# When the beacon keys of the last five sequences are loaded, cast and turned, in a fused attention and MLP kernel

## The chip, the cores and the metric

The kernel runs on one core of one Trainium2 chip. The metric is device time in microseconds (us) of one execution, and the time before is the median of three runs. A profile is one execution recorded by the hardware profiler. The engines are PE (TensorE matmul; its weight loads are shown as PEld), DVE (VectorE), ACT (ScalarE), POOL (GpSimd) and SP (SyncE, which here only issues DMAs). Every engine works through its own list of instructions in order.

## The reference

The first half is attention over 8 sequences with 8 heads of 64, 576 tokens each. Ahead of the causal keys stand 16 "beacon" keys and values per head that every token sees. The second half is an MLP over the 4608 tokens.

```python
k_all = np.concatenate([beacon_k, k], axis=2)          # 16 + 576 keys, B=8, H=8, D=64
v_all = np.concatenate([beacon_v, v], axis=2)
scores = scale * np.matmul(q, k_all.transpose(0, 1, 3, 2))
scores = np.where(causal, -1000000000.0, scores)       # no mask on the beacons
...
x = np.ascontiguousarray(attn_out.transpose(0, 2, 1, 3)).reshape(B * S, H * D)
h = x @ w_in                                           # 512 -> 2048
g = np.maximum(0.01 * h, h)
return (g @ w_out).astype(np.float32)                  # 2048 -> 512
```

## The kernel before

**Tiling.** Two heads make a pair, so there are 32 pairs, g = 0 to 31, four to a sequence. A pair's keys stand in one of eight buffers, `k_bufs[g % 8]`, as 64+64 rows (two heads) by 592 columns: 16 beacon columns first, then the 576 keys. Scores are made transposed, keys by queries, in 64-row matmuls (`score` at L267 for pairs 0 to 7, `stretch` at L314 for pairs 8 to 31); ACT takes the exponential (L276, L329, L333); POOL zeroes the causal triangles (`triangle`, L289; called the masks here); the value matmuls (L359) also give the sums, and DVE divides (L388, L389). The MLP runs in nine chunks of 512 tokens between these steps: `up` is one 128-column piece of the first product (L442, then ACT's Prelu at L450), `down` a piece of the second (L519 for the first chunk, L544 after it, in a seven-product scheme whose sums DVE makes at L785).

**How keys get into place.** For pairs 8 and up, `load_natural` (N, L171) issues two DMAs on POOL's queue for q (N g.0) and two for k (N g.1), which also cast to bf16; `turn_pair` (T, L179) issues two DMA transposes on SP's queue that write qT and columns 16 to 591 of the key buffer. `load_v_cast` (L209, L214) loads values on POOL's queue.

**Beacon keys.** They take a path of their own. `load_beacon_k(b0, b1, eng)` (L185) loads a range of sequences as fp32, 128 partitions (head, beacon) by sequence by 64, one packet of 256 bytes for each row. `cast_beacon_k` (L188) casts to bf16. `beacon_transposes` (L194) does two PE transposes for each sequence into one PSUM tile, and DVE copies the result in two halves into `bkT` (L203). `beacon_columns` (step b, L229) is a POOL copy of 16 columns of `bkT` into pair g's key buffer. Sequences 0 and 1 (pairs 0 to 7) go a separate, early way, and the rest, sequences 2 to 7 (pairs 8 to 31), are loaded, cast and turned together.

**The order of work.** Up to pair 7 the order is written out by hand in strings that `run` reads: s score, m mask, v value, x finish, l, N and V loads, T turn, q and k transposes on PE, b beacon columns, u up, d down, o a half of w_out. From pair 8 (`FIRST`) on, the order is a list of events, each with a due time counted in pairs and a priority; `block(m)` is three score tiles of 512 columns for each head with their masks behind them. The list is sorted, and before each event the loop calls `fill()`, which emits ups and downs until their count reaches what is due at that time. So an event's time says between which ups and downs PE meets it, and in which order POOL, DVE and SP meet their own parts. Pair 12 first appears in block 4 (due 12.09), pair 13 in block 5 (13.02), pair 14 in block 6 (13.94) and pair 15 in block 7 (14.86).

**PSUM.** One pool, `ps_one`, has four banks. Ups, values, the first tile of each block (two banks) and the transposes share them in turn: a new tile takes the bank of the fourth tile before it and waits until that has been read out.

Of the kernel before, what the change touches and what calls it, by code (L numbers as in the profile page):

```python
# [15 lines left out]
def kernel(  # L16
# [11 lines left out]
    nc = tc.nc  # L28

    B, H, S, D = q.shape  # L30
# [5 lines left out]
    NPAIR = H // 2  # L36
# [80 lines left out]
    def make_pads():  # L117
        nc.vector.memset(k_all[:, :, NB + S :], 0.0)
        for t in a_bufs:
            for c in PADS:  # L120
                nc.vector.memset(t[:, :, c : c + 48], 0.0)

    def make_ones():
        for t in v_bufs:
            nc.vector.memset(t[:, :, :, D : D + 1], 1.0)
# [37 lines left out]
    def load_first_keys():  # L163
        for h in range(2):
            nc.sync.dma_start(out=first_k[h], in_=k[0, h].rearrange("(p i) d -> p i d", i=RI))
# [18 lines left out]
    def load_beacon_k(b0, b1, eng):  # L184
        eng.dma_start(out=bk_raw[:, b0:b1], in_=beacon_k[b0:b1].rearrange("b h n d -> (h n) b d"))  # L185

    def cast_beacon_k(b0, b1, copy):
        copy(out=bk[:, b0:b1], in_=bk_raw[:, b0:b1])  # L188

    def beacon_transposes(b0, b1):  # L190
        ps = ps_one.tile([128, 1024], BF16, name="tp", tag="one")
        for b in range(b0, b1):
            for par in range(2):
                nc.tensor.transpose(  # L194
                    ps[par * 64 : par * 64 + 64, (b - b0) * 128 : (b - b0 + 1) * 128], bk[:, b], ident
                )
        for par in range(2):
            ps_ = slice(par * 64, par * 64 + 64)
            src = ps[ps_, 0 : (b1 - b0) * 128].rearrange("p (x e n) -> p e x n", e=2, n=NB)[:, par]
            if b0 == 0:  # L200
                nc.vector.tensor_copy(out=k_all[ps_, :, 0:NB], in_=src)
            else:
                nc.vector.tensor_copy(out=bkT[ps_, b0:b1].rearrange("p b h n -> p (b h) n"), in_=src)  # L203
# [134 lines left out]
    def triangles(parts):  # L338
        for g, lo, hi in parts:
            for c in range(NKB):  # L340
                n = (112, 128, 128, 128, 80)[c]
                if lo < FLAT[c] + n <= hi:
                    triangle(probs[g], FLAT[c], n, ROWS[c])
# [167 lines left out]
    def ND(i):  # L511
        return NF if i == 0 else 2 * len(PRODUCTS)
# [308 lines left out]
    def unused(n, cols=128):  # L821
        ps = ps_one.tile([128, 512], FP32, name="av", tag="one")
        r, w = max(1, cols // 128), min(cols, 128)
        for i in range(n):
            nc.tensor.matmul(
                out=ps[:, 0 : r * w].rearrange("p (r w) -> p r w", w=w),
                lhsT=blank,
                rhs=blank[:, None, 0:w].to_broadcast([128, r, w]),
                start=True,
                stop=True,  # L830
            )
# [82 lines left out]
    with order:  # L914
        load_first_keys()
        load_beacon_k(0, 2, nc.scalar)
        nc.vector.memset(blank, 0.0)
        nc.vector.memset(ident, 0.0)
        run("l0.0 l1.0")
        make_identity(nc, ident, nomemset=True)  # L920
        make_ones()
        run("l1.1 l2.0 l2.1 V0.0 V0.1 l3.0 l3.1 V0.2 V0.3 V0.4 l4.0 l4.1 i0")
        make_pads()
        unused(13, 256)
        cast_beacon_k(0, 2, nc.scalar.copy)
        beacon_transposes(0, 2)
        unused(13)
        nc.scalar.copy(out=k_nat0[:, :, 0], in_=first_k[0])
        nc.vector.tensor_copy(out=k_nat0[:, :, 1], in_=first_k[1])
        run("q0.1 k0 w2.384 s0.0 m0.0 w3.256 s0.1 q1 s0.2 m0.1 k1 s0.3 m0.2")  # L930
        run("w2.384 s1.0 m1.0 q2 s1.1 k2 w2.384 s1.2 m1.1 w2.384 s1.3 m1.2 W0.0.4 s2.0 m2.0 W0.0.4 s2.1 W0.0.6 q3 l5.0 l5.1 s2.2 k3 w4.384 v0.0 m2.1 s2.3 i1 m2.2 W0.1.4 s3.0 m3.0 v1.0 s3.1 v0.1 s3.2 v1.1 m3.1 l6.0 l6.1 s3.3 x0.1 m3.2")
        run("v2.0 V1.0 V1.1 q4 v2.1 x1 k4.1 v3.0 v3.1 x2.1 s4.0 s4.1 x3 m4.0 V1.2 V1.3 V1.4 l7.0 l7.1 u u s4.2 s4.3 q5 k5 m4.1 m4.2 u o0 u")
        load_beacon_k(2, B, nc.gpsimd)
        run("s5.0 s5.1 m5.0 u u u s5.2 s5.3 q6 k6 m5.1 m5.2 o1 u u s6.0 s6.1 m6.0 u v4.0 u v4.1 y4 N8.0 N8.1 u s6.2 s6.3 q7 k7 m6.1 m6.2 u")
        cast_beacon_k(2, B, nc.gpsimd.tensor_copy)
        run("u v5.0 u v5.1 N9.0 s7.0 s7.1 m7.0 d x5 v6.0 v6.1 T8 d s7.2 s7.3")
        beacon_transposes(2, B)
        run("m7.1 m7.2 N9.1 u b8.2 b9.2 b10.2 b11.2 x6 v7.0 T9 v7.1 d d d N10.0 N10.1 d V2.0 V2.1 x7 t0 T10")


        FIRST = 2 * NPAIR
        COLS = FLAT[NKB]
        TILES = (NG - FIRST) * COLS // 512

        def tile_parts(n):
            at, end, parts = 512 * n, 512 * (n + 1), []
            while at < end:
                r, lo = divmod(at, COLS)
                hi = min(COLS, lo + end - at)
                parts.append((FIRST + r, lo, hi))  # L950
                at += hi - lo
            return parts

        def block(m):
            tiles = [tile_parts(n) for n in range(3 * m, min(3 * m + 3, TILES))]
            for n, parts in enumerate(tiles):
                stretch(parts, apart=n == 0)
            for parts in tiles:
                triangles(parts)

        def has_down():
            return at2[0] < done1[0] // NF

        since = 0
        events = []
        for g in range(FIRST, NG):
            if g > FIRST + 2:
                events.append((g - 3.25, 0, run, ("N%d.0" % g,)))
                events.append((g - 2.95, 0, run, ("N%d.1" % g,)))
            if g > FIRST + 2:  # L970
                events.append((g - 1.75, 0, run, ("T%d" % g,)))
            if g > FIRST + 3:
                events.append((g - 2.5, 0, run, ("b%d.2" % g,)))
            at = g + (2.05 if g % NPAIR == NPAIR - 1 else 2.25)
            events.append((at, 3, value, (g, 0)))
            events.append((at + 0.37, 4, value, (g, 1)))
            if g < NG - 1:
                events.append((at + 0.38, 5, x_turn, (g,)))
        for m in range((TILES + 2) // 3):
            events.append((FIRST + (0.4 if m else 0.6) + 1536 / COLS * m, 2, block, (m,)))  # L980
        ends = [FIRST]
        for g in range(FIRST, NG):
            at = g + (2.5 if g == NG - 1 else 3.5)
            events.append((at, 2, finish, (g, 2)))
            if g % NPAIR == NPAIR - 1:
                ends.append(at)
        for at, n in ((NG - 1.2, 5), (NG - 0.3, 6), (NG + 0.7, 4)):
            events.append((at, 7, w_in_sums, (n,)))
        for b in range(2, B):
            for n in range(2 if b == 2 else 0, NKB):  # L990
                events.append((4 * b + ((-0.1, 0.1)[n > 3] if b == 2 else 0.3 * n - 0.4), 6, load_v_cast, (b, n)))
        events.sort(key=lambda e: e[:2])
        first_down[0] = 4
        w, d0 = 0, done1[0] + done2[0]
        for at, _, what, args in events:
            while w + 2 < len(ends) and at > ends[w + 1]:
                w, d0 = w + 1, done1[0] + done2[0]
            todo = NF * ready[0] + sum(ND(i) for i in range(ready[0])) - (KEPT if w + 2 < len(ends) else LEFT) - d0
            aim = d0 + todo * (at - ends[w]) / (ends[w + 1] - ends[w])
            while done1[0] + done2[0] < aim and fill():  # L1000
                pass
            if what is block:
                since = done1[0] + done2[0]
            elif what is value:
                while done1[0] + done2[0] < since + (2 if has_down() else 4) and fill(True):
                    pass
            what(*args)
        assert at2 == [TAIL - 1, ND(TAIL - 1) - LEFT] and done1[0] == TAIL * NF, (at2, done1)
        apart_from_values[0] = True
        last_chunks("D X31 x7 d a1 R111 x8 R111 t u d u d u d u u d u d u u w")  # L1010
        last_chunks("R111 R111 R111 t u d u d u d u d d d14")
# [30 lines left out]
```

## Time and profile before

| what | value |
|---|---|
| median of three runs (lowest, highest) | 325.34 us (325.18, 329.55) |
| the profiled execution's own time | 325.64 us |
| its span, first to last instruction | 323.8 us |
| time outside of the span | 1.84 us |
| granted TensorE clock | 1.00 |
| PE busy | 314.3 us (97%) |
| POOL busy | 184.3 us (57%) |
| ACT busy | 203.8 us (63%) |
| packets on POOL's DMA queue | 99824 |

The span is what lies between the first and the last instruction. Busy times are a union over an engine's instructions. A timeline line has the start, the time covered, engine, line, operation, tile written and tile read, shape and count, and in brackets the idle time before it and what ended that. Times in it are from the start of the span. In the chain of waits, a line is a start, a length and what the time belonged to.

### The profile page before, as it was taken

What the parts mean: (1) busy time and instruction counts of PE and PEld (TensorE: products, weight loads), DVE (VectorE), ACT (ScalarE), POOL (GpSimd) and SP (SyncE); (2) the same over time, 40 slices, a digit from 0 to 9 for tenths busy, and PEclk for the clock granted to TensorE, in tenths of its full rate; (3) what the DMA queues carried; (4) which work ended last, traced back from release to release, by engine and by line L of the source; (5) the groups of instructions that cost most, each with busy time, mean ns of one, the idle gap of its engine ahead of it and who ended that gap; (6) DMA issues with size and microseconds to landing.
All of it is one profiled execution on the core that took longest, in us unless ns stands there. A gap on an engine that the chain in (4) does not pass through costs nothing.

```text
span 323.8 us, 8701 instructions
## 1 busy us (share of the span) xinstructions
PE 314.3 (97%) x3468; PEld 219.1 (68%) x3494; DVE 168.0 (52%) x341; ACT 203.8 (63%) x346; POOL 184.3 (57%) x354
## 2 busy tenths in 40 slices
PE   7999999999999999999999999999999999999995
PEld 4575555444588557855788888656875697688784
DVE  3464245508255244444443454525464689577954
ACT  4968962387855786478746874687458547455510
POOL 8895868999996787659875977666221000000000
PEclk9999999999999999999999999999999999999999
DMA  8999999999999999999999999999222100200123
GB/s 137 129 189 192 124 214 140 169 177 188 135 152 160 216 138 129 114 186 97 141 176 174 99 143 119 188 128 129 44 81 82 26 2 32 75 25 2 65 67 130
DMA packets 155256, 39.78 MB, mean 123 GB/s; under 512 B 142368, under 2 KB 152480, under 8 KB 155216
## 3 DMA queue, kind: packets, MB, share of 16 engines
q0 software_dynamic: 99824, 18.54, 91.1%
q1 hardware_dynamic: 55120, 20.62, 38.3%
q8 instruction: 27, 0.44, 0.6%
q14 instruction: 13, 0.11, 0.1%
q10 hardware_dynamic: 272, 0.07, 0.1%
HBM read 37.22 MB, written 9.44 MB: 144 GB/s over the span
## 4 chain that ended last, share of the span: by engine, by line
PE 72%; DMA 14%; POOL 9%; ACT 3%; issue 1%; DVE 0%; POOLq 0%; ACTq 0%; SPq 0%
PE acc L442 24%; PE acc L544 19%; PE sc L544 11%; PE av L359 6%; PE sc L314 5%; PE acc L663 5%; DMA w_out_sb<-in_moe_w_out_dram 4%; DMA gsum<-in_k_dram 4%; POOL aT L289 3%; DMA k_nat<-in_k_dram 3%; DMA v_aug<-in_v_dram 2%; ACT aT L333 2%; DMA kT<-k_nat 2%; POOL gsum L158 1%; POOL v_aug L214 1%
## 5 line engine op out<-in xcount | busy, mean ns | idle before, releaser
L442 PE MATMUL acc<-xT,w_in_sb 128*128 128x512 bf16 (+1 forms) x537 | 116.5, 354 | 1.5 <-ACT aT L329 0.3
L450 ACT ACTIVATE gT<-acc 128x512 bf16<-128x512 f32 x124 | 70.8, 623 | 33.1 <-PE acc L442 32.6
L289 POOL TENSOR_SCALAR_AFFINE_SELECT aT<-aT 128x256 bf16<-128x256 bf16 (+2 forms) x160 | 59.7, 403 | 51.4 <-ACT aT L329 31.5
L442 PEld LDWEIGHTS <-w_in_sb 128*128 128x128 bf16 x560 | 51.7, 98 | 43.9 <-issue 2.9
L544 PEld LDWEIGHTS <-gT 128*128 128x128 bf16 x512 | 48.7, 98 | 7.7 <-issue 1.8
L333 ACT ACTIVATE aT<-sc 128x1024 bf16<-128x1024 f32 (+3 forms) x64 | 51.7, 892 | 0.0
L329 ACT ACTIVATE aT<-sc 128x512 bf16<-128x512 f32 (+3 forms) x64 | 29.0, 520 | 27.8 <-PE sc L314 27.8
L388 DVE RECIPROCAL rec<-av 128x6 f32<-128x6 f32 (+1 forms) x64 | 12.0, 187 | 65.0 <-PE av L359 64.4
L359 PEld LDWEIGHTS <-aT 128*128 128x128 bf16 (+1 forms) x960 | 36.9, 98 | 9.2 <-issue 1.4
L544 PEld LDWEIGHTS <-gsum 128*128 128x128 bf16 x384 | 36.5, 98 | 6.5 <-issue 0.4
L359 PE MATMUL av<-v_aug,aT 128*128 128x65 bf16 (+1 forms) x960 | 39.8, 194 | 0.8 <-DMA v_aug<-in_v_dram 0.4
L214 POOL DMA_DIRECT2D v_aug<-in_v_dram x40 | 34.1, 856 | 4.2 <-DMA w_in_sb<-in_moe_w_in_dram 3.8
L171 POOL DMA_DIRECT2D k_nat<-in_k_dram x48 | 34.8, 730 | 0.9 <-DMA w_out_sb<-in_moe_w_out_dram 0.3
L171 POOL DMA_DIRECT2D q_nat<-in_q_dram x48 | 34.8, 729 | 0.6 <-issue 0.4
L389 DVE TENSOR_TENSOR x_nat<-av,rec 128x384 bf16<-128x384 f32 (+1 forms) x64 | 31.4, 491 | 2.2
L544 PE MATMUL acc<-w_out_sb,gT 128*128 128x256 bf16 x240 | 28.9, 273 | 0.4 <-ACT gT L450 0.4
L276 ACT ACTIVATE aT<-sc 128x1024 bf16<-128x1024 f32 (+3 forms) x32 | 26.0, 874 | 4.7 <-PE sc L267 2.5
L314 PE MATMUL sc<-qT,kT 64*128 64x80 bf16 (+22 forms) x384 | 22.2, 250 | 0.3
L314 PEld LDWEIGHTS <-kT 64*128 64x128 bf16 x384 | 12.8, 94 | 11.2 <-issue 7.6
L544 PE MATMUL acc<-w_sum,gsum 128*128 128x256 bf16 x160 | 20.1, 273 | 0.0
L575 ACT COPY p<-acc 128x512 f32<-128x512 f32 x15 | 9.1, 604 | 16.8 <-PE acc L544 16.8
L785 DVE TENSOR_TENSOR gsum<-gT 128x1024 bf16<-128x1024 bf16 x16 | 11.0, 688 | 15.7 <-ACT gT L450 15.7
(95 smaller groups left out, 339.0 us busy)
## 6 DMA issues: line engine op xcount, KB each, us to landing
out_dram<-p SPq DMA_DIRECT2D x26, 256.0 KB, 3.2
q_nat<-in_q_dram POOLq DMA_DIRECT2D x48, 72.0 KB, 5.5
k_nat<-in_k_dram POOLq DMA_DIRECT2D x48, 72.0 KB, 5.3
v_aug<-in_v_dram POOLq DMA_DIRECT2D x24, 128.0 KB, 6.5
w_in_sb<-in_moe_w_in_dram POOLq DMA_DIRECT2D x2, 1024.0 KB, 12.4
w_out_sb<-in_moe_w_out_dram POOLq DMA_DIRECT2D x2, 1024.0 KB, 12.1
out_dram<-u SPq DMA_DIRECT2D x8, 256.0 KB, 2.7
gsum<-in_q_dram POOLq DMA_DIRECT2D x8, 144.0 KB, 7.1
```

The source lines that it names most:

```text
L171: nc.gpsimd.dma_start(out=t[:, :, par], in_=(q, k)[which][b, 2 * hp + par].rearrange("(t p) d -> p t d", p=NR),)
L214: nc.gpsimd.dma_start(out=dst[lo : ROWS[c], c, :, 0:D], in_=v[b, :, OFF[c] : OFF[c] + n].rearrange("h p d -> p h d"),)
L276: nc.scalar.activation(out=aT[:, :, c0 : c0 + w], in_=sc[:, :, 0:w], func=AF.Exp, scale=0.125)
L289: nc.gpsimd.affine_select(out=view, in_=view, compare_op=ALU.is_ge, fill=0.0, base=128 - n if lo == 0 else 0, channel_multiplier=-1, patte ...
L314: nc.tensor.matmul(out=(sc[par] if apart else sc[:, par])[:, at : at + b - a], lhsT=kT[ps_, c * 128 : (c + 1) * 128], rhs=qT[ps_, q0 : q0 ...
L329: nc.scalar.activation(out=probs[g][:, par, lo:hi], in_=sc[par][:, at : at + hi - lo], func=AF.Exp, scale=0.125)
L333: nc.scalar.activation(out=probs[g][:, :, lo:hi], in_=sc[:, :, at : at + hi - lo], func=AF.Exp, scale=0.125)
L359: nc.tensor.matmul(out=avv[:, n, 0 : D + 1], lhsT=aT[0 : ROWS[c], par, a0 : a0 + 128], rhs=va[0 : ROWS[c], c, 2 * hp + par, :], start=(c = ...
L389: nc.vector.tensor_tensor(out=x_nat[:, t0:t1].rearrange("p t e d -> p (t e) d"), in0=avv[:, :, 0:D], in1=rec[:, n0:n1, None].to_broadcast( ...
L442: nc.tensor.matmul(out=acc[:, lo:hi], lhsT=w_in_cols(fc, j), rhs=xT[:, j, x0 : x0 + hi - lo], start=(j == 0), stop=(j == NJ - 1), skip_gro ...
L450: nc.scalar.activation(out=gT[i][:, fc, :], in_=acc, func=AF.Prelu, alpha=0.01)
L544: nc.tensor.matmul(out=acc[:, lo : lo + HD], lhsT=left(i, n, fc, tile), rhs=right(n, fc), start=(lo == 0 and fc == 0), stop=(fc == HF - 1) ...
```

## The change

The early load, cast and turn take sequence 2 alone (pairs 8 to 11). Sequences 3 to 7 get a second load, due at 9.85 (in POOL's list between the q and the k loads of pair 13, N13.0 and N13.1), a second cast, due at 11.45 (in POOL's list behind the masks of block 3), and second transposes with their DVE copies, due at 11.6 (in PE's list between the two halves of pair 9's values). The beacon columns of pairs 12 to 15, which were due 2.5 pairs ahead of their pair, are due 0.38 ahead, since `bkT` is filled only now; those of pairs 16 and up stay where they were. Work as such is the same, apart from one DMA, one cast, one PSUM tile and two DVE copies more, each of these on fewer columns than the single one before.

```diff
-        load_beacon_k(2, B, nc.gpsimd)
+        load_beacon_k(2, 3, nc.gpsimd)
...
-        cast_beacon_k(2, B, nc.gpsimd.tensor_copy)
+        cast_beacon_k(2, 3, nc.gpsimd.tensor_copy)
...
-        beacon_transposes(2, B)
+        beacon_transposes(2, 3)
...
             if g > FIRST + 3:
-                events.append((g - 2.5, 0, run, ("b%d.2" % g,)))
+                events.append((g - (2.5 if g >= FIRST + 2 * NPAIR else 0.38), 0, run, ("b%d.2" % g,)))
...
+        events.append((FIRST + 1.85, 0, load_beacon_k, (3, B, nc.gpsimd)))
+        events.append((FIRST + 3.45, 0, cast_beacon_k, (3, B, nc.gpsimd.tensor_copy)))
+        events.append((FIRST + 3.6, 0, beacon_transposes, (3, B)))
         events.sort(key=lambda e: e[:2])
```

## The prediction

> **What bounds the kernel now.** I read the page first: busy times, slices and queues.
>
> ```profile
> PE 314.3 (97%) x3468; PEld 219.1 (68%) x3494; DVE 168.0 (52%) x341; ACT 203.8 (63%) x346; POOL 184.3 (57%) x354
> ...
> POOL 8895868999996787659875977666221000000000
> ...
> DMA  8999999999999999999999999999222100200123
> ...
> q0 software_dynamic: 99824, 18.54, 91.1%
> ```
>
> PE is the bound: 9.5 of 323.8 us are not PE's, and they include the head and the tail. So a microsecond that PE stands still is a microsecond of the end, and work that moves within PE's list costs nothing. But POOL and the DMA engines are full for the first two thirds, which is where the change works. Next, the chain of waits there.
>
> ```profile
> 39.96 13.69 DMA w_out_sb<-in_moe_w_out_dram
> ...
> 64.21 8.28 DMA k_nat<-in_k_dram
> 72.49 0.02 SPq L179
> 72.51 0.03 issue
> 72.54 5.26 DMA kT<-k_nat
> 77.80 0.05 issue
> 77.85 0.67 PE sc L314 x10
> ```
>
> Up to 77.85 the chain runs through POOL's loads; from there on nearly all is PE. So what could be won lies ahead of 77.85, and only as far as PE really waits. The timeline of PE, PEld's row among it:
>
> ```profile
> 77.12 1.39 PE L314 MATMUL sc<-qT,kT 64*128 64x96 bf16 x16
> 77.84 0.39 PEld L314 LDWEIGHTS <-kT 64*128 64x128 bf16 x10 [0.32 <-DMA kT<-k_nat]
> 81.91 1.13 PE L359 MATMUL av<-v_aug,aT 128*128 128x65 bf16 x30
> 83.83 0.83 PE L314 MATMUL sc<-qT,kT 64*128 64x224 bf16 x12
> 90.28 0.85 PE L314 MATMUL sc<-qT,kT 64*128 64x16 bf16 x16
> ```
>
> Block 3 (77.12) waits 0.32 us for pair 11's turned keys: the late transfer is worth only that. 81.91 is pair 9's values, both halves (12 and 18 matmuls, 0.031 us each, the second half from 82.32), where the new transposes go between. 83.83 is block 4, which needs pair 12; 90.28 is block 5, which needs pair 13. Last, the timeline of POOL:
>
> ```profile
> 48.15 0.50 POOL L188 CAST bk<-bk_raw 128x384 bf16<-128x384 f32 x1 [2.78 <-DMA bk_raw<-in_beacon_k_dram]
> ...
> 53.94 0.72 POOL L171 DMA_DIRECT2D k_nat<-in_k_dram  x1 [0.34 <-DMA w_out_sb<-in_moe_w_out_dram]
> ...
> 80.53 1.38 POOL L289 TENSOR_SCALAR_AFFINE_SELECT aT<-aT 128x256 bf16<-128x256 bf16 x4
> 81.87 0.19 POOL L229 COPY kT<-bkT 128x16 bf16<-128x16 bf16 x1
> ```
>
> POOL has no idle time between 72.6 and 97.6: each thing put into its list there makes all behind it later. The 80.53 row is block 3's masks, behind which the new cast stands.
>
> **The early stage.** Ten of twelve transposes leave 50.73 (0.45 us for twelve, start to start, so 0.0375 each): PE is 0.37 us ahead. The load has 128 packets in place of 768. By the landings of single issues, the first half of w_out lands at 47.26, the beacon load at 48.09, so its 768 packets take 0.83 us; 640 fewer are 0.69 us. The cast still waits for that landing behind w_out, until about 47.4; what POOL wins there is lost again at 51.70, where it waits for ACT (0.92 us). The wait at 53.94 is for the second half of w_out, issued eight POOL DMAs earlier and landed at 53.65; it then lands near 52.96, and POOL, free at 53.60, goes on 0.34 sooner. Two more waits look the same, for loads issued eight before: 0.28 us at 69.53 (landing 69.24) and 0.17 at 72.61 (landing 72.32). Loads land 0.34 to 0.69 sooner, I take 0.5, so pair 13's second q load is issued at 72.0 in place of 72.61, with pair 12's copy (a step of 0.13) gone too. Pair 11's keys are turned at 77.3 in place of 77.80. Block 0 (61.15, right behind pair 8's turned keys at 61.06) moves with its keys. So PE is 0.5 us ahead behind block 3: the gain so far.
>
> **The load.** One more issue on POOL, ahead of pair 13's k. The value load of 640 packets (64.93) takes 0.76 us on POOL, bounds 0.53 (beacon values, 58.06) and 0.85 (today's 768 packets). It goes out at 72.73. Issues from 71.71 to 74.05 landed after 4.97 to 5.73 us, so it lands at 77.7 to 78.5, more than 3 us ahead of the cast. The transfers behind it lose the 0.69 us again, to about today's times: pair 13's keys were turned at 89.18, and block 5 asks for them past 90.5. SP's list gets nothing new.
>
> **A rule against the load.** The DVE sums at L468 to L470 took 1.22 to 1.23 us each (57.98 to 61.71), and the five POOL issues that start beside them (58.06 to 61.02) 0.53 to 0.91 as elsewhere, so I add nothing for DVE. The Trainium skill, "SBUF — State Buffer", section "SBUF: two separate sides", says that a DVE operation holding the port pair it shares with GpSimd keeps GpSimd from writing descriptors. By that the issue beside the L472 sum could wait up to 2.30 us, and the total would be about 3 us in place of 0.65; the five issues speak against it. What did collide there is a mask: the third of block 2's (75.41) took 1.44 us beside L472, its kind elsewhere 0.38. POOL and DVE shift against each other now, so those 1.05 us stay or go; I keep them, and take the other end for a rival.
>
> **The cast.** At the end of block 3's masks POOL is 0.61 ahead, less 0.76 for the load, plus 0.13 for pair 13's copy, which goes: 0.02 late, so the cast starts at 81.89. It costs 0.50 x 320/384 = 0.42 us (bounds 0.19, the smallest POOL copy, and 0.50): done 82.31, seen by PE about 0.05 later as at 77.80 to 77.85, and 82.40 with rounding up.
>
> **The transposes.** PE is done with the first half of pair 9's values at 82.28 - 0.5 = 81.78 and now waits 0.6 us: POOL, not PE, sets this point. Behind the wait stand the second half, one up and block 4. Ten transposes take 0.375 us, so the second half starts at 82.78, where it was 82.32: the gain of 0.5 is gone and 0.46 us are lost. Its PSUM bank is that of the third up instead of the second; ACT read that out at 82.76 at the latest, and now sooner, so nothing is added. DVE's two copies (0.36 each for 384 columns, so at most 0.7) end near 83.55. Behind them on DVE stands the second half's division, which SP's x transposes take at 84.81 (it was done at 83.82; covered).
>
> **Pair 12 to 15's columns.** Behind the cast come two value loads (82.00 to 83.34), then pair 12's copy, 83.65 to 83.84. Block 4 needs it at 84.06 + 0.46 = 84.52: covered by 0.68. POOL is now 0.44 late (0.42 cast, 0.02). Pair 13's copy stood at 77.53 and now stands behind block 4's masks and two value loads: today's 89.70, plus 0.44, plus the load of 0.86, so 91.00 to 91.19. Block 5's fifth group of matmuls, which needs it, was at 90.59, now 91.05; with 0.05 to be seen, PE waits 0.19. Pair 14's copy comes at 96.6 to 96.8, block 6 needs it past 97.4; for pair 15 POOL has had idle time since 97.6. Block 4's masks get 0.44 late, but pair 11's values, which need them, come 4 us later.
>
> **Sum.** +0.46 + 0.19 = 0.65 us. Nothing behind absorbs it: PE's own wait rows sum to 4.0 us over the whole span, and most of that is ahead of 78. On the profiled execution that is 325.64 + 0.65 = 326.3; the median lies 0.30 below that execution, so 326.0. A measurement of this kernel tells about 2% (6.5 us) from no change, so I call this the same.
>
> **A rule on splitting.** The packets take 0.83 us per 768 between landings that follow each other, so cutting one load in two adds only the issue. The Trainium skill, "DMA: Bandwidth & Descriptors", section "Anatomy of one DMA — SWDGE (gpsimd) path", gives each DMA a fixed 2 us, mostly completion; as occupancy it would make the sum about 2.6, and landings half a microsecond apart (54.33, 54.69, 55.32, 55.70) say it is not that.
>
> **Rival 1, the relief pays.** If the 1.05 us of the slow mask go, POOL no longer sets the point: block 3's last mask then waits for ACT (81.29 - 0.5), the cast ends near 81.7, PE does not wait, the second half starts at its bank's release, 82.76 - 0.5 = 82.26, and pair 13's copy is in time. That is -0.06, so 325.3; and if the DMAs land the full 0.69 sooner with no bank in the way, at best -0.6, 324.7. For it: rows of 0.38 for that mask everywhere else. Against: POOL is full. Chance 0.33.
>
> **Rival 2, the landing takes the place of the cast's early wait (slower).** The load's own row today is 10.65 us to land, waiting at 48.15 for 2.78. At 72.73 + 10.65 = 83.38 POOL would stand 1.5 us at the cast, PE with it, and pair 13's copy goes as late: 0.65 + 1.5 = 2.15, 327.5. With the longest landing of the trace, 13.69, it is 5.2, 330.5. It decides from 9.2 us on (81.89 - 72.73). Against: issues from 60 to 100 landed within 8.83. Chance 0.1.
>
> **Rival 3, POOL's copies late one after another.** If the load and cast cost their upper ends (0.09 and 0.08 more) and one more mask collides for 1.05, PE waits 1.2 more at the transposes and pair 13's stall stays: 1.9, 327.2. Chance 0.1.
>
> **How the numbers follow.** The forecast's own case (0.2 to 1.5 us slower, 325.5 to 326.8) gets 0.47, the rivals 0.33, 0.1 and 0.1. The range goes from rival 1's best, 324.7, less 0.2 as runs scatter, 324.5, to rival 2's first price, 327.5, with 0.3 for scatter (median to profiled execution): 327.8. Left out are rival 2 with longer landings and a run disturbed like the 329.55 one. Over 2% slower needs 6.5 us, which only rival 2's worst with rival 3's 1.25 on top would reach: 0.03, out of theirs. Over 2% faster would need more than PE's waits hold: 0.01.
>
> **What will show it.** Right: PE's transposes in two places, the second behind a wait on POOL's cast of some tenths; the wait for pair 11's kT smaller; POOL's row at 53.94 without its wait; the cast with no DMA wait. Wrong: a cast that waits for its load; transposes with no wait (rival 1); masks of 1.4 us in new places; a wait of block 4 on pair 12's copy; or landings that did not move.

## The result

The changed kernel is slower by a little: over 22 runs of each, 1.0047 of the time before, with a 95% interval of 1.0027 to 1.0066. The medians are 327.08 and 325.27 us. The medians count every execution, the ratio leaves out the slow ones (more than 1.5% above the kernel's fastest). At 325.3 us the ratio is 1.5 us, from 0.9 to 2.1. That is inside 2% and slower, as forecast, but more than twice the 0.65 us of the prediction, which lies below the interval.

The page of the changed kernel, in the lines that answer to those shown of before:

```profile
PE 321.2 (98%) x3468; PEld 222.0 (67%) x3494; DVE 168.1 (51%) x343; ACT 204.5 (62%) x346; POOL 185.1 (56%) x356
...
POOL 8857874999998778756966887678221000000000
...
DMA  8999999999999999999999999999422100100123
...
q0 software_dynamic: 99856, 18.54, 81.2%
```

In this one execution PE's matmuls were much slower up to about 24 us, ahead of every instruction that the change touches (two unused matmuls of 384 columns took 0.82 us, in before 0.50; the profile's granted clock is 1.00 in both). Its span is 329.3 us, so the readings below use a second profile of the same kernel, e_again, with a span of 325.0 us. The counts of the page hold: two POOL instructions, two DVE copies and 32 packets more.

The timeline of PE in e_again (start, time covered, instructions, idle time before):

```profile
76.84 0.34 PE L314 MATMUL sc<-qT,kT 64*128 64x96 bf16 x6
77.82 0.67 PE L314 MATMUL sc<-qT,kT 64*128 64x128 bf16 x10 [0.63 <-DMA kT<-k_nat]
81.88 0.53 PE L359 MATMUL av<-v_aug,aT 128*128 128x65 bf16 x12
82.34 0.47 PE L194 MATMUL tp<-ident,bk 128*64 128x128 bf16 x10
82.78 0.71 PE L359 MATMUL av<-v_aug,aT 128*128 128x65 bf16 x18
84.29 0.83 PE L314 MATMUL sc<-qT,kT 64*128 64x224 bf16 x12
90.74 0.47 PE L314 MATMUL sc<-qT,kT 64*128 64x16 bf16 x10
91.88 0.56 PE L314 MATMUL sc<-qT,kT 64*128 64x384 bf16 x6 [0.66 <-POOL kT L229]
```

Three things are to be seen. The wait for pair 11's turned keys in block 3 is still there and larger (0.63 us on PE's row and 0.82 on PEld's, where before has 0.32; PE goes on at 77.82, before at 77.85). The ten transposes at 82.34 wait for nothing, and push the second half of the values from 82.32 to 82.78. And block 5 breaks off after ten matmuls and waits 0.66 us for pair 13's beacon columns.

POOL beside it:

```profile
79.67 1.01 POOL L289 TENSOR_SCALAR_AFFINE_SELECT aT<-aT 128x256 bf16<-128x256 bf16 x3
81.33 0.41 POOL L289 TENSOR_SCALAR_AFFINE_SELECT aT<-aT 128x256 bf16<-128x256 bf16 x1 [0.65 <-ACT aT L333]
81.69 0.45 POOL L188 CAST bk<-bk_raw 128x320 bf16<-128x320 f32 x1
...
83.86 0.20 POOL L229 COPY kT<-bkT 128x16 bf16<-128x16 bf16 x1 [0.44 <-DVE bkT L203]
84.38 1.44 POOL L171 DMA_DIRECT2D q_nat<-in_q_dram  x2 [0.32 <-issue]
...
91.60 0.22 POOL L229 COPY kT<-bkT 128x16 bf16<-128x16 bf16 x1
```

The cast comes at 81.69 and waits for no load. Pair 12's copy waits 0.44 us for DVE's copies of the transposes, the next issue another 0.32 us, and so pair 13's copy, at the end of this list, is at 91.60, when PE could have used it from 91.05 on.

**One number for all that follows.** From the moment PE goes on in block 3, with its seventh matmul, to the end of the span, nothing of the early stage counts any more, and where PE was held at that point the stretch repeats within a few hundredths of a microsecond from profile to profile. It says nothing of what lies ahead of that point, which in the profiles other than the result's stands anywhere from 76.6 to 79.1 us. Before it is 245.91 us (323.76 - 77.85), in e_again 247.22: 1.31 us more. From going on in block 3 to the start of block 4 it is 5.99 before and 6.48 in e_again (0.49 more, the transposes); from block 4 to block 6 12.63 and 13.47 (0.84 more, the wait at block 5 with its restart). 0.49 + 0.84 = 1.33, and behind block 6 both take 227.3 us. Below, "the stretch" is the first of these, "3 to 4" and "4 to 6" the others.

### The profile page after: what moved, and what is told of

It is laid out like the page before. It is cut to its first block, busy times and chain, and to the rows that moved or that the text cites. A ratio compares the mean times of both kernels' runs of the same rounds, so it can differ in the third digit from the quotient of the medians.

```text
span 329.3 us, 8709 instructions
## 1 busy us (share of the span) xinstructions
PE 321.2 (98%) x3468; PEld 222.0 (67%) x3494; DVE 168.1 (51%) x343; ACT 204.5 (62%) x346; POOL 185.1 (56%) x356
## 4 chain that ended last, share of the span: by engine, by line
PE 91%; POOL 3%; ACT 3%; issue 1%; DVE 0%; ACTq 0%; POOLq 0%
PE acc L442 29%; PE acc L544 19%; PE sc L544 11%; PE av L359 8%; PE sc L314 6%; PE acc L663 5%; PE acc L519 4%; PE sc L267 3%; PE av L825 3%; PE tp L243 2%; ACT aT L333 1%; POOL v_aug L214 1%; POOL aT L289 1%; ACT aT L329 1%; POOL k_nat L171 1%
## 5 line engine op out<-in xcount | busy, mean ns | idle before, releaser
L333 ACT ACTIVATE aT<-sc 128x1024 bf16<-128x1024 f32 (+3 forms) x64 | 51.7, 892 | 0.0
L276 ACT ACTIVATE aT<-sc 128x1024 bf16<-128x1024 f32 (+3 forms) x32 | 26.8, 874 | 9.0 <-PE sc L267 8.6
L785 DVE TENSOR_TENSOR gsum<-gT 128x1024 bf16<-128x1024 bf16 x16 | 11.0, 688 | 16.5 <-ACT gT L450 16.4
```

The lines of the kernel that those rows point to most:

```text
L276: nc.scalar.activation(out=aT[:, :, c0 : c0 + w], in_=sc[:, :, 0:w], func=AF.Exp, scale=0.125)
L333: nc.scalar.activation(out=probs[g][:, :, lo:hi], in_=sc[:, :, at : at + hi - lo], func=AF.Exp, scale=0.125)
```

## The experiments

**The same kernel again (e_again)**, no edit.

> The changed kernel once more, for a profile whose first 25 us are not disturbed and for the size of the loss. Theory: the loss is two waits of PE, 0.53 us for POOL's cast and 0.56 us for pair 13's beacon columns, less about 0.3 us that the earlier loads give back; from PE's first beacon transposes of the second group (50.73 before) to block 6 (96.47 before) it takes 46.5 us where before took 45.74, and behind that nothing differs: 0.8 us in all. Rival: the 1.5 us of the comparison are right and half of them lie elsewhere, ahead of or behind that stretch; then the stretch is 46.5 again but the span is 1.5 us over that of before.

Measured 1.008 (1.0045 to 1.0115) of before; the profile is that above. The theory failed in its first half: the wait for the cast, 0.53 us in the result's own profile, is gone. Here POOL was early enough to stand 0.65 us waiting for ACT ahead of block 3's last mask, and the cast was done at 82.14, ahead of PE's 82.34; in the other profile the four masks ran without a break and the cast started 0.8 us later, counted from PE's going on in block 3. So that wait comes and goes with the early stage; what stays is the transposes' own time and block 5. The 1.31 us of the stretch are 1.0040, inside the result's interval but below this run's.

**The cast ahead of block 3's masks (e_cast_early).**

```diff
-        events.append((FIRST + 3.45, 0, cast_beacon_k, (3, B, nc.gpsimd.tensor_copy)))
+        events.append((FIRST + 3.1, 0, cast_beacon_k, (3, B, nc.gpsimd.tensor_copy)))
```

> The cast moves from behind block 3's masks to ahead of them in POOL's list. Theory: POOL reaches it 1.5 us sooner, by when the load has landed for over 1 us, so the cast ends before PE needs it: PE's 0.53 us at the transposes go, pair 13's wait of 0.56 us grows by about as much as PE comes sooner (POOL's list up to that copy is the same in sum), so the time stays within 0.2 us of the changed kernel. Rival (the two waits are independent): 0.5 us less than the changed kernel.

Measured 1.0064 (1.0044 to 1.0084). The stretch is 247.22, 3 to 4 is 6.48, 4 to 6 13.47: the same as e_again in all three. In neither of the two profiles does PE wait for the cast, so its place costs nothing there. The run times (1.0064 and 1.008) lie 0.5 us apart with intervals wider than that, so how often the cast holds PE in other executions stays open.

**The columns of pairs 13 to 15 with pair 12's (e_cols_early).**

```diff
-  events.append((g - (2.5 if g >= FIRST + 2 * NPAIR else 0.38), 0, run, ("b%d.2" % g,)))
+  events.append((g - 2.5 if g >= FIRST + 2 * NPAIR else FIRST + 3.62, 0, run, ("b%d.2" % g,)))
```

> The beacon columns of pairs 13 to 15 are copied with pair 12's, right behind the late transposes, in place of 0.38 ahead of their pair. Theory: the wait of 0.56 us at block 5 goes and nothing takes its place; the wait of 0.53 us for the cast stays: 0.5 us less than the changed kernel. Rival (POOL's lateness sets block 5 in any case, through the turned keys or the masks): no change.

Measured 1.0029 (1.0006 to 1.0052). Block 5 runs through:

```profile
77.15 0.67 PE L314 MATMUL sc<-qT,kT 64*128 64x128 bf16 x10 [1.63 <-DMA kT<-k_nat]
81.22 0.53 PE L359 MATMUL av<-v_aug,aT 128*128 128x65 bf16 x12
81.68 0.47 PE L194 MATMUL tp<-ident,bk 128*64 128x128 bf16 x10
82.12 0.71 PE L359 MATMUL av<-v_aug,aT 128*128 128x65 bf16 x18
83.63 0.83 PE L314 MATMUL sc<-qT,kT 64*128 64x224 bf16 x12
90.08 0.85 PE L314 MATMUL sc<-qT,kT 64*128 64x16 bf16 x16
```

All 16 matmuls of block 5 stand in one line, and 4 to 6 is 12.63 as before. The stretch is 246.38: 0.84 us less than e_again, and the 0.47 us that are left are the transposes. PE came to block 3 two microseconds sooner than in before (75.18) and waited 1.63 us there: all but 0.7 us of its lead is lost. (The lead itself is not shown to be the edit's: it is there at block 0 already, at 59.18 for 61.15.)

**Without the late steps (e_no_late).** Leaves out the second load, cast, transposes and DVE copies; pairs 12 to 31 get sequence 2's columns.

```diff
-        events.append((FIRST + 1.85, 0, load_beacon_k, (3, B, nc.gpsimd)))
-        events.append((FIRST + 3.45, 0, cast_beacon_k, (3, B, nc.gpsimd.tensor_copy)))
-        events.append((FIRST + 3.6, 0, beacon_transposes, (3, B)))
...
-        copy(out=k_bufs[g % NK][:, 0:NB], in_=bkT[:, b, hp])
+        copy(out=k_bufs[g % NK][:, 0:NB], in_=bkT[:, min(b, 2), hp])
```

> Leaves out part of the computation: the second load, cast, transposes and copies, so that pairs 12 to 31 get sequence 2's beacon columns, at the due times of before. What is left is the early relief alone. Theory: no wait of PE at either place, ten transposes (0.375 us) less and the waits at blocks 0 and 3 (0.29 and 0.32 us) gone: the stretch takes 44.8 to 45.1 us, and the time is 0.6 to 1.0 us less than before. Rival (the early packets were hidden): only the transposes' 0.4 us less. Rival (the loss lies in the early stage, in code or queue order): not less than before.

Measured 1.0006 (0.9978 to 1.0034), the stretch 245.91, exactly before's. The early relief is worth nothing that shows here (the interval would still allow a gain of 0.7 us), and even ten transposes left out altogether bring nothing. In the profile the relief is lost before block 3, at block 0, in PE's rows of before and then of this kernel:

```profile
61.15 0.85 PE L314 MATMUL sc<-qT,kT 64*128 64x512 bf16 x12
```

```profile
61.33 0.85 PE L314 MATMUL sc<-qT,kT 64*128 64x512 bf16 x12 [0.80 <-DVE w_sum L470]
77.31 0.34 PE L314 MATMUL sc<-qT,kT 64*128 64x96 bf16 x6
78.24 0.67 PE L314 MATMUL sc<-qT,kT 64*128 64x128 bf16 x10 [0.59 <-DMA kT<-k_nat]
```

The bracket names a DVE operation, but pair 8's turned keys landed at 61.24, and block 0 starts 0.09 us behind that landing in every profile except the result's and that of e_cols_early (before: 61.06 and 61.15, after an idle time of 0.12). PE had done what stands ahead by 60.53, half a microsecond sooner than in before (61.02), and the keys came no sooner. From block 0 to block 3 it is 16.0 us in every kernel that puts no other PE work between them, so what is won ahead of block 0 has no way to block 3 while these keys come no sooner.

**Is the wait at block 3 a gate?** Three unused matmuls of 512 columns, 0.65 us, in the kernel before, once ahead of block 3 and once where the change has its transposes.

```diff
+        events.append((FIRST + 2.9, 0, unused, (3, 512)))     # e_pad_ahead
+        events.append((FIRST + 3.6, 0, unused, (3, 512)))     # e_pad_behind
```

> The kernel before, with three unused matmuls of 512 columns (some 0.65 us of PE) put into PE's list between blocks 2 and 3, ahead of the wait for pair 11's turned keys. Theory (that wait is a gate, and what PE does ahead of it is covered as far as the wait goes): the wait, 0.32 us in the profile of before and 0.6 to 1.6 in those of the last three kernels, shrinks by as much, and the end moves by 0 to 0.35 us. Rival (PE's list simply adds up): the end moves by 0.65 us and the wait stays.

> The kernel before, with the same three unused matmuls between the halves of pair 9's values, where the change puts its transposes. Theory: nothing covers them there; from block 3's wait to block 4 it takes 0.65 us more, and the end moves by 0.65 us. Rival (the wait for a PSUM bank at that place covers part of it): less than 0.3 us.

Measured 0.9997 (0.9966 to 1.0028) ahead and 1.0014 (0.9988 to 1.004) behind. The times can't tell these two apart. The stretches are 245.94 ahead and 246.57 behind, against 245.91, but padding ahead lies outside of the stretch, so its 245.94 is no measure of it. In PE's timelines, first ahead, then behind:

```profile
76.65 0.81 PE L825 MATMUL av<-blank 128*128 128x512 bf16 x3
77.30 1.02 PE L442 MATMUL acc<-xT,w_in_sb 128*128 128x512 bf16 x4
78.26 0.83 PE L314 MATMUL sc<-qT,kT 64*128 64x96 bf16 x16
```

```profile
76.00 0.34 PE L314 MATMUL sc<-qT,kT 64*128 64x96 bf16 x6
77.07 0.67 PE L314 MATMUL sc<-qT,kT 64*128 64x128 bf16 x10 [0.73 <-DMA kT<-k_nat]
...
81.55 0.81 PE L825 MATMUL av<-blank 128*128 128x512 bf16 x3
```

Behind, the wait stands and the padding comes on top, 0.66 us for 0.65: that side of the theory is shown. Ahead, block 3 is one line of 16 and the wait is gone, but the padding did not fill it: in this execution pair 11's turned keys landed at 76.81, and PE, even without padding, would have come to its seventh matmul at 77.79. From block 0 to block 3 it took 16.62 us, 0.65 more, so here the padding was paid in full. What the profiles do show is the wait as a gate: in eight of them PE, coming to block 3 anywhere from 75.18 to 77.31, waits there and goes on 0.04 to 0.05 us behind the keys' landing. That work is covered as far as such a wait goes follows from this; by how much differs from execution to execution.

**The late columns alone (e_cols_late_only)**, in the kernel before.

```diff
-  events.append((g - 2.5, 0, run, ("b%d.2" % g,)))
+  events.append((g - (2.5 if g >= FIRST + 2 * NPAIR else 0.38), 0, run, ("b%d.2" % g,)))
```

> The kernel before, with the beacon columns of pairs 12 to 15 copied 0.38 pairs ahead of their pair as in the change, and nothing else changed. Theory (POOL's lateness from the load and the cast makes most of pair 13's wait of 0.66 us): the wait at block 5 is 0 to 0.3 us and the end moves by as much. Rival (the copy's place alone does it): the whole 0.5 to 0.7 us.

Measured 1.0014 (0.9989 to 1.0039). The rival's size was right: the stretch is 246.66, 0.75 us more, and 4 to 6 is 13.37, with no load and no cast in the way. The copy itself took longer there:

```profile
89.70 0.65 POOL L229 COPY kT<-bkT 128x16 bf16<-128x16 bf16 x1
```

Beside it DVE makes the sums of L785 without a break (88.30 to 90.90), and the copy ends 0.05 us behind one of them; in before 21 of the 24 copies of this kind took 0.19 to 0.25 us and three 0.68 to 0.75. With 0.2 us the copy would have left PE a wait of about 0.1 us. So the same wait is made in two ways: here the copy starts 0.32 us behind block 5 (89.38) and is slow; in e_again it starts 0.86 behind and takes 0.22. The place leaves pair 13 almost no room; POOL's lateness, or a slow copy, does the rest.

**The late steps ahead of the gate (e_before_gate).**

```diff
-        events.append((FIRST + 1.85, 0, load_beacon_k, (3, B, nc.gpsimd)))
-        events.append((FIRST + 3.45, 0, cast_beacon_k, (3, B, nc.gpsimd.tensor_copy)))
-        events.append((FIRST + 3.6, 0, beacon_transposes, (3, B)))
+        events.append((FIRST + 0.7, 0, load_beacon_k, (3, B, nc.gpsimd)))
+        events.append((FIRST + 2.2, 0, cast_beacon_k, (3, B, nc.gpsimd.tensor_copy)))
+        events.append((FIRST + 3.1, 0, beacon_transposes, (3, B)))
...
-  events.append((g - (2.5 if g >= FIRST + 2 * NPAIR else 0.38), 0, run, ("b%d.2" % g,)))
+  events.append((g - 2.5 if g >= FIRST + 2 * NPAIR else FIRST + 3.12, 0, run, ("b%d.2" % g,)))
```

> The change with its late steps moved ahead of the wait for pair 11's turned keys: load ahead of pair 12's q, cast ahead of block 2's masks, transposes between blocks 2 and 3, columns of pairs 12 to 15 right behind them. Theory: the ten transposes are covered by the wait at block 3, pair 13's copy is long done, and the losses of 0.45 and 0.66 us behind that wait are both gone: within 0.4 us of before, 1 us less than the change. If POOL has to wait for the load at the cast, block 2's masks come later by some tenths, which costs nothing, as their values come over 4 us later. Rival (the loss is the split itself: one DMA, one cast, one PSUM tile more): as slow as the change.

Measured 1.0002 (0.9979 to 1.0025): level with before, and its interval lies below the result's ratio. The split as such (one DMA, one cast, one PSUM tile more) costs nothing that can be seen (by the interval, 0.8 us at most). 3 to 4 is 5.99 and 4 to 6 is 12.63, both as before. Of the transposes' 0.41 us ahead of block 3 the wait covered about half: the keys landed at 76.59, PE's seventh matmul is at 76.84, and without transposes PE would have been there at 76.43. The stretch is 247.14 all the same, since in the one profile PE then met the next transfer, behind block 6:

```profile
100.11 0.53 PE L359 MATMUL av<-v_aug,aT 128*128 128x65 bf16 x12
101.72 0.35 PE L359 MATMUL av<-v_aug,aT 80*128 80x65 bf16 x6 [1.07 <-DMA v_aug<-in_v_dram]
```

Here the third sequence's last values land at 101.68, before at 99.52, as block 4's five masks took 3.56 us on POOL (before 1.73) ahead of their issue. So block 3 is not the only gate; a microsecond saved at one can be lost at the next.

**The whole load back in its early place (e_load_whole, e_whole_2), and the change a third time (e_small_2).**

```diff
-        load_beacon_k(2, 3, nc.gpsimd)
+        load_beacon_k(2, B, nc.gpsimd)
...
-        events.append((FIRST + 1.85, 0, load_beacon_k, (3, B, nc.gpsimd)))
```

> The change with the whole load (sequences 2 to 7) back in its early place; cast, transposes and columns stay split as in the change. Open is why pair 11's turned keys land 14.4 to 15.0 us after the second issue of their k load in the profiles with the small early load, and 13.05 to 14.2 in those with the whole one. Theory (the place of the transposes and pair 13's copy make the loss, the load does nothing): from PE's going on at block 3 to the end 246.4 to 247.2, that is 0.45 to 1.2 us over before, as the copy comes 0.75 us sooner in POOL's list; the landing stays as scattered. Rival (the small early load itself makes these keys late): the landing is back at 13.0 to 14.2 us and the time is nearer to before by some tenths.

> The changed kernel once more, for one more landing of pair 11's turned keys. If the small early load itself delays them, they land 14.4 to 15.0 us after the second issue of their k load, as in four profiles with it; if that was scatter, anywhere from 13.0 to 15.0. From PE's going on at block 3 to the end 247.2 in both.

> The change with the whole early load once more, for the same number: 13.0 to 14.2 us if the place of the load matters, 13.0 to 15.0 if it was scatter.

Measured 1.003 (1.0011 to 1.0049) for e_load_whole; e_small_2 and e_whole_2 were one run each. The stretches are 247.53, 247.23 and 247.27 (in the first PE was not held at block 3, and waited 0.34 us for a PSUM bank at the transposes instead): without a late load the loss behind the gate is that of the change, so the late load is not its cause; that the copy would come 0.75 us sooner did not happen. It starts 0.64 and 0.89 us behind block 5 (0.86 in e_again): in e_whole_2 pair 12's copy and the issue behind it wait as in e_again (0.26 and 0.32 us), and in e_load_whole block 3's masks took 2.25 us. From the second issue of pair 11's k load to the landing of its turned keys it took 13.04 to 14.17 us in the seven profiles with the whole early load, 14.39 to 15.0 in the five with the small one and the late load of the change or none, leaving aside the disturbed profile of the result (12.91) and e_before_gate (13.63), whose second load goes out ahead of these keys. The two groups do not overlap, which speaks against scatter, but two of the seven profiles with the small load had to be left aside for it, so a cause is not shown. Counted from the beacon load's issue, the second half of w_out lands on average 0.8 us sooner with the small load, pair 10's k 0.5 us sooner, and pair 11's k 0.4 us later, all three with groups that overlap.

**Less behind the gate (e_block3_12)**, in the kernel before: block 3 due 0.12 pairs later, which puts one up and half of pair 9's values ahead of it.

```diff
-  events.append((FIRST + (0.4 if m else 0.6) + 1536 / COLS * m, 2, block, (m,)))
+  events.append((FIRST + (0.4 if m else 0.6) + 1536 / COLS * m + (0.12 if m == 3 else 0), 2, block, (m,)))
```

> The kernel before, with block 3 due 0.12 pairs later: one up and the first half of pair 9's values (0.86 and 0.37 us of PE) come ahead of the wait for pair 11's turned keys instead of behind it. Theory (that wait is a gate): the wait of 0.3 to 0.8 us goes, nothing is added behind it, 0.3 to 0.7 us less than before; from PE's going on at block 3 to the end 1.2 us less than the 245.91 of before. Rival: the next wait for a transfer takes the gain back (as pair 12's values waited for the value load when the transposes stood ahead of block 3): no change.

Measured 0.9998 (0.9974 to 1.0021): no gain, as the rival said. The wait at block 3 is gone, and of the 1.23 us moved 1.08 have left the stretch (244.83), as work put ahead of it must. Only the wait itself could be won. In this execution that was about 0.2 us: the keys landed at 76.86, and PE would have come to its seventh matmul at 76.69 without the moved work. What the rival named, a next wait that takes the gain back, is not in this profile: PE has no wait for a transfer behind block 3. No version here beats the kernel before by more than its interval.

## Why the prediction was right, and where its steps were not

- **Right: the forecast as a whole, with luck in its sum.** Within 2% and slower, with POOL's lateness and the transposes as the cause. The result's 1.5 us lies at the upper end of the forecast's own case (0.2 to 1.5), and the median of 327.08 past it but inside the range; the runs told it from no change, where the prediction took 2% for the least that can be told. The late load lands in time, as forecast (issued 72.57, landed 77.74 in e_again, 4 us ahead of the cast), and the transposes push the second half of the values to 82.78, the number forecast, though by luck, as the next point says.
- **Wrong: "work that moves within PE's list costs nothing".** This holds only where no outside wait lies between the two places. The waits at block 0 and at block 3 lie between 50.73 and 82.34. Behind block 3's the transposes cost 0.47 to 0.49 us, and padding of 0.65 us there cost 0.66; leaving them out ahead of block 0 brought nothing. The 0.46 us of the sum was right in size by luck: it was made of a gain of 0.5, a wait of 0.6 for the cast and 0.375 of transposes. In e_again the first two are not there, and they nearly cancel. In the result's profile the wait for the cast is (0.53 us), as forecast, but that execution lost 4 us ahead of it.
- **Wrong: "loads land 0.34 to 0.69 sooner, I take 0.5", and the 0.5 us that PE should be ahead behind block 3.** The relief exists where it was worked out (POOL goes on without its wait at 53.94; w_out's second half lands 0.8 us sooner on average), but it does not reach block 3. PE meets block 0 first and waits there for pair 8's keys: 0.63 to 0.85 us in four of the five undisturbed profiles with the small load (leaving aside e_before_gate), 0.12 in before's. And pair 11's turned keys do not land sooner. PE goes on in block 3 at 77.82, before at 77.85, and e_no_late, with the relief alone, has before's time.
- **Mis-sized: pair 13's copy, 0.19 us, measured 0.84.** Up to the cast the count on POOL was 0.2 us off (81.69 for 81.89). Then two waits were missing from the sum: DVE's copies of the transposes were taken to end at 83.55, ahead of POOL; they ended at 83.81, and POOL waited 0.44 us for them, and 0.32 us more ahead of the next issue. That is 84.38 for 83.78, and with it 91.60 for 91.00. PE's need was forecast at 91.05, and there it is: block 5 starts at 90.74, and its fifth group stands 0.31 behind.
- **Rival 1 had its condition met** (block 2's third mask took 0.37 us in e_again, in before 1.44, and block 3's last one waits for ACT, as it says) and not its price: the transposes ran without a wait for the cast, but no gain of 0.5 us stood behind them, and pair 13's copy was late all the same. **Rival 2** did not occur. **Rival 3's** place, POOL's copies late one after another, was the right one for half of the loss.
- **The rule against the load** (the Trainium skill, "SBUF — State Buffer", "SBUF: two separate sides"): the late issue took 0.93 us in the result's profile, against 0.76 taken, which is nowhere near a wait for a DVE sum. The prediction read the rule too widely: the section speaks of DVE's two-port modes and says, as an inference, that an operation on two tensors, as these sums are, takes only the pair's read side, and descriptor writing needs the write side. The issues agree. What grew beside DVE's sums were POOL's own operations: a copy in e_cols_late_only (0.65 us for 0.2) and masks in e_before_gate (3.56 us for five, in before 1.73).
- **Open:** whether and why pair 11's keys land later with less ahead of them; how often PE waits for the cast; and the few tenths between the 1.31 us of the stretch and the 1.5 us of the result, which the later landing may or may not be.

## What to carry to other kernels

Before calling a move within the bounding engine's list free, look for a wait on something outside between the old and the new place: ahead of such a gate work is covered as far as the wait goes, behind it it is paid for. To price what lies behind a gate, measure from the gate to the end rather than over the span: here that tells 0.1 us, where the runs tell 0.5. For what lies ahead of it this measure is blind, and a gain there counts only if the transfer itself lands sooner. And when a producer's step is put just ahead of its user, count the whole relay (cast, transpose, copy out, copy in) with each engine's wait for the one before it, since every engine behind in its list passes that wait on to all that stands behind it.

## What the runs showed of the hardware

In twelve of the fourteen profiles, less load ahead did not mean an earlier landing: with 640 packets fewer in the queue the keys of pair 11 took 14.4 to 15.0 us from issue to turned, with them 13.0 to 14.2; the other two, with the small load, 12.9 and 13.6, don't fit.

A POOL copy of 16 columns took about 0.2 us. But where it overlapped one of DVE's sums of two SBUF tensors (L785), it ended 0.05 to 0.07 us behind the end of such a sum, however long that made it: 59 of 60 such copies in the fourteen profiles, which took 0.21 to 0.75 us. A mask took 1.44 us for 0.38 beside the sum of L472. The q and k issues on POOL took 0.72 to 0.78 us, beside such sums or not.
